# Squares of 32x32 on VectorE in place of 128x128 transposes on TensorE, from block 4 on

## The chip, the cores and the metric

The kernel runs on one core of one Trainium2 chip. The metric is the device time of one execution in microseconds (us). The engines are TensorE (PE), VectorE (DVE), ScalarE (ACT), GpSimd (POOL) and SyncE (SP), which here only issues transfers; each runs its own instructions in a fixed order, and they meet through semaphores.

## The reference

Attention against keys and values that are averaged over groups of 8 tokens, then a layer with a rational function in the middle. All in float32: 8 sequences of 576 tokens, 8 heads of 64; 4608 tokens, 512 model columns, 2048 hidden columns.

```python
k_p = k.reshape(B, H, Sp, pool, D).mean(axis=3)          # Sp = 72, pool = 8
v_p = v.reshape(B, H, Sp, pool, D).mean(axis=3)
scores = scale * np.matmul(q, k_p.transpose(0, 1, 3, 2))
scores = scores - np.max(scores, axis=-1, keepdims=True)
attn = np.exp(scores)
attn = attn / (np.sum(attn, axis=-1, keepdims=True) + 1e-09)
x = np.matmul(attn, v_p)                                  # then (B*S, H*D)
h = x @ w_in
P = a[0] + a[1] * h + a[2] * h2 + a[3] * h3               # h2 = h*h, h3 = h2*h
Q = 1.0 + np.abs(b[0]) * np.abs(h) + np.abs(b[1]) * h2
return (P / (Q + 1e-6)) @ w_out
```

## The kernel before

**Blocks and units.** The 4608 tokens are cut into 18 blocks of 256 (TOK), a block into two tiles t of 128, the 2048 hidden columns into 8 units u of 256. Sequences have 576 tokens, so some blocks straddle two of them; `segs` cuts such a block or tile in two. For a block i, `attend(i)` makes x; for each unit `mm1` multiplies x with w_in into ph, `rational` makes g from it, and `mm2` multiplies g with w_out into po, which gathers over the 8 units. Float32 products are made from high and low halves (names ending in 0 and 1, or gh and gl, am[0] and am[1]: high, and what is left).

**Attention of a tile** (`attention`). q arrives as rows of tokens (qt, one transfer of 256 KB, two when the tile straddles). PE transposes it in four 128x128 pieces into a bank pq, ACT copies that to qT. PE multiplies qT with the averaged keys kpT (ps), DVE takes the maxima mx and the differences e, ACT the exponentials, DVE the sums sm, POOL divides. e then has 72 keys for each of 8 heads, stored as 4 pairs of heads of 144 columns. The first 16 columns of a pair go their own way (er, pr, ar). The other 128 are transposed by PE into a bank pm; ACT copies it to the block's high half am[0], DVE subtracts to get the low half am[1]. `values` multiplies am and ar with the averaged values (pv), giving x.

**A unit's rational function** (`rational`). On ACT: w = Abs, r, t (both linear), then Ln and Exp into rp, then the cast gh. On DVE five instructions that end in t. On POOL the products w and gl.

**What sets the order.** Nothing is scheduled by the compiler: `Plan` records every operation with a cost in us and a due time, and `solve` places them engine by engine, taking the operation that can start first, by due time where several can. Due times come from `due(at)` (HEAD, PACE, SLOW) for the unit in which a block's work is recorded, and go backwards along the dependencies with a factor `slack`; `early` is how long before its due time an operation may start. A transfer is charged its issue cost and its bytes. `issue` then emits that order, so all instructions have line L240, and an instruction whose operand is late holds up all behind it on its engine. All transfers are issued by SP, in one queue.

Of the kernel before, what the change touches and what calls it, by code (L numbers as in the profile page):

```python
# [99 lines left out]
class Plan:  # L100
    LAT = 0.07

    def __init__(self, nc):
        self.nc, self.ops, self.rings, self.now, self.slack = nc, [], {}, 0.0, 1.2
# [10 lines left out]
    def add(self, eng, cost, calls, port=False, claims=(), bytes=0, early=24.0, after=()):  # L115
# [143 lines left out]
def tile_pooled_attention_then_rational_moe(  # L259
# [67 lines left out]
    def dma(kbytes, dst, src, eng="sp", issue=0.45, early=60.0):  # L327
        plan.add(eng, issue, [("dma_start", (dst, src), {})], bytes=kbytes * 1024, early=early)
# [232 lines left out]
    def attention(t, am, ar):  # L561
# [3 lines left out]
        qt = new("work2", "qt", [P, H, D], F32, f"qt{t}")  # L565
        for r0, r1, n in sg:
            s0 = t * P + r0 - n * S
            dma(512, qt[r0:r1], q[n, :, s0:s0 + (r1 - r0), :].rearrange("h s d -> s h d"))
        pq = bank(f"pq{t}", [P, NJ, P])
        qT = new("work1", "qT", [P, NJ * P], F32, f"qT{t}").rearrange("p (j t) -> p j t", j=NJ)  # L570
        pe(109 * NJ, [
            ("transpose", (pq[:, j, :],
                           qt[:, 2 * j:2 * j + 2, :].rearrange("s h d -> s (h d)"), ident), {})
            for j in range(NJ)], claims=(qT,))
# [4 lines left out]
        for c in range(2):
            hs = slice(4 * c, 4 * c + 4)  # L580
            ps = bank(f"ps{t}_{c}", [P, 4, SP])
# [242 lines left out]
```

## Time and profile before

| | us |
|---|---|
| median of the runs (3) | 979.89 |
| lowest and highest run | 977.5, 981.26 |
| profiled execution | 975.84 |
| span of the profiled execution | 974.1 |
| PE busy in the span | 957.4 |
| DVE, ACT, POOL busy | 735.0, 707.0, 504.9 |

Matmuls overlap: the duration of one is not what it takes from PE's queue, the distance between two starts is. PE busy thus says that something was always in it. The granted clock is TensorE's, as a share of 2.4 GHz.

### The profile page before, as it was taken

Reading aid. Unit: us, or ns where it says so; the run is one execution under the profiler, and the core shown is the slowest. Engines: PE = TensorE matmul, PEld = TensorE weight load, DVE = VectorE, ACT = ScalarE, POOL = GpSimd, SP = SyncE. Lnnn points to the kernel's source line nnn. Section 1 sums busy time; section 2 is a strip of 40 time slices with the busy share of each in tenths; the row PEclk is TensorE's granted clock in tenths of the full one; section 3 lists DMA queues with packets and bytes.
Section 4 is the critical chain, followed back from the end, with each engine's and each line's share of the span. In section 5 each row is a group of like instructions: output and inputs, shape, how many; then the busy total and the mean of one; then the engine's idle time right before and its main releaser. Section 6 shows DMA issues by size and latency. Waiting matters only on the chain.

```text
span 974.1 us, 16916 instructions
## 1 busy us (share of the span) xinstructions
PE 957.4 (98%) x6396; PEld 868.4 (89%) x6396; DVE 735.0 (75%) x1299; ACT 707.0 (73%) x1216; POOL 504.9 (52%) x443
## 2 busy tenths in 40 slices
PE   7899999999999999999999999999999999999997
PEld 6888999989898999999899989898999999999996
DVE  5898878888777768776888687867777785767664
ACT  3888889776777777777677776767776776777764
POOL 4475567664445644444645373446544474444343
PEclk9899999999999999999999999999999999999999
DMA  9993001251102301010401040102201210100000
GB/s 272 328 387 138 22 23 44 88 151 50 29 23 65 87 12 33 17 34 11 125 18 44 6 131 29 40 4 66 87 17 34 54 56 11 35 1 22 2 23 22
DMA packets 62706, 64.26 MB, mean 66 GB/s; under 512 B 39969, under 2 KB 39969, under 8 KB 62625
## 3 DMA queue, kind: packets, MB, share of 16 engines
q1 hardware_dynamic: 62624, 63.19, 20.8%
q8 instruction: 50, 0.82, 0.3%
q14 instruction: 32, 0.25, 0.1%
HBM read 50.60 MB, written 12.58 MB: 65 GB/s over the span
## 4 chain that ended last, share of the span: by engine, by line
PE 91%; DVE 3%; SPq 2%; ACT 1%; issue 1%; POOL 1%; DMA 1%; POOLq 0%; ACTq 0%; DVEq 0%
PE ph L240 40%; PE po L240 39%; PE pv L240 4%; PE ps L240 3%; SPq L240 2%; PE pq L240 1%; PE pm L240 1%; DVE t L240 1%; DMA qt<-in_q_dram 1%; PE warm L240 1%; POOL wout L240 0%; PE pr L240 0%; DVE m_wout L240 0%; PE pvs L240 0%; DVE rp L240 0%
## 5 line engine op out<-in xcount | busy, mean ns | idle before, releaser
L240 PEld LDWEIGHTS ph<-x,win 128*128 128x128 f32 x3264 | 475.3, 188 | 54.2 <-DVE vr L240 0.9
L240 PE MATMUL ph<-x,win 128*128 128x256 f32 x3264 | 502.6, 283 | 0.8 <-DVE vr L240 0.7
L240 PE MATMUL po<-wout,gh 128*128 128x512 f32 x1152 | 352.9, 397 | 0.7 <-ACT gh L240 0.7
L240 POOL TENSOR_TENSOR w<-w,r 128x512 f32<-128x512 f32 x144 | 187.5, 1302 | 271.6 <-ACT r L240 268.7
L240 POOL TENSOR_TENSOR gl<-t,gh 128x512 fp32r<-128x512 f32 x144 | 189.8, 1318 | 152.3 <-ACT gh L240 108.0
L240 PEld LDWEIGHTS po<-wout,gh 128*128 128x128 f32 x1152 | 182.7, 189 | 9.4 <-ACT gh L240 1.2
L240 DVE TENSOR_TENSOR t<-t,ph 128x512 f32<-128x512 f32 x144 | 98.4, 683 | 119.4 <-ACT t L240 111.0
L240 PE MATMUL po<-wout,gl 128*128 128x512 f32 x576 | 177.1, 396 | 0.5 <-POOL gl L240 0.5
L240 DVE SCALAR_TENSOR_TENSOR t<-t,abn,rp 128x512 f32<-128x512 f32 x144 | 106.9, 742 | 47.5 <-ACT rp L240 46.6
L240 ACT ACTIVATE w<-ph 128x512 f32<-128x512 f32 x144 | 85.8, 596 | 69.5 <-PE ph L240 65.7
L240 ACT ACTIVATE rp<-w,cbias 128x512 f32<-128x512 f32 x144 | 99.4, 691 | 38.8 <-POOL w L240 23.8
L240 ACT CAST gh<-t 128x512 fp32r<-128x512 f32 x144 | 88.6, 615 | 48.1 <-DVE t L240 47.9
L240 ACT ACTIVATE r<-w,abn 128x512 f32<-128x512 f32 x144 | 117.6, 816 | 8.1 <-DVE rp L240 2.3
L240 ACT ACTIVATE t<-ph,abn 128x512 f32<-128x512 f32 x144 | 109.8, 772 | 16.0 <-PE ph L240 12.7
L240 DVE SCALAR_TENSOR_TENSOR t<-t,abn,ph 128x512 f32<-128x512 f32 x144 | 107.4, 746 | 6.9 <-ACT w L240 2.7
L240 DVE SCALAR_TENSOR_TENSOR t<-rp,t 128x512 f32<-128x512 f32 x144 | 99.1, 688 | 3.9
L240 DVE SCALAR_TENSOR_TENSOR rp<-w,rp 128x512 f32<-128x512 f32 x144 | 98.9, 687 | 0.1
L240 PEld LDWEIGHTS po<-wout,gl 128*128 128x128 f32 x576 | 91.6, 189 | 6.0 <-POOL gl L240 1.8
L240 ACT ACTIVATE rp<-rp 128x512 f32<-128x512 f32 x144 | 84.1, 584 | 3.4
L240 POOL TENSOR_TENSOR e<-e,sm 128x576 f32<-128x576 f32 x36 | 40.9, 1154 | 15.0 <-DVE sm L240 15.0
L240 PE MATMUL pv<-am,vm 128*128 128x256 f32 (+3 forms) x288 | 46.8, 283 | 0.7 <-DVE am L240 0.7
L240 PE MATMUL ps<-kpT,qT 128*128 128x144 f32 (+1 forms) x320 | 44.7, 292 | 1.8 <-DVE t L240 0.8
(88 smaller groups left out, 864.2 us busy)
## 6 DMA issues: line engine op xcount, KB each, us to landing
out_dram<-ob SPq DMA_DIRECT2D x18, 512.0 KB, 2.8
qt<-in_q_dram SPq DMA_DIRECT2D x32, 256.0 KB, 3.2
rwin<-in_moe_w_in_dram SPq DMA_DIRECT2D x8, 1024.0 KB, 10.6
rwout<-in_moe_w_out_dram SPq DMA_DIRECT2D x8, 1024.0 KB, 11.3
st_k<-in_k_dram SPq DMA_DIRECT2D x12, 512.0 KB, 4.0
st_v<-in_v_dram SPq DMA_DIRECT2D x12, 512.0 KB, 3.9
st_v<-in_v_dram SPq DMA_DIRECT2D x48, 64.0 KB, 2.3
early<-in_k_dram SPq DMA_DIRECT2D x4, 512.0 KB, 8.9
```

Of the source, the lines that this page charges most:

```text
L240: getattr(engines[op.eng], name)(*map(value, args), **{k: value(v) for k, v in kw.items()})
```

## The change

For blocks 4 to 17 (tiles 8 to 35) neither q nor the softmax's weights pass through PE's transposes.

- **q.** `squares(i)` loads q into a tile qs of squares, [128, 4, 8, 32], by 16 transfers per sequence in the block: each fills 32 partitions with runs of 32 floats (128 bytes). One DVE instruction per tile transposes sixteen 32x32 squares straight into qT. pq and ACT's copy go. Blocks 0 to 3 keep the old way, their qt now a part of the same buffer.
- **Weights.** e becomes one tile es per block. After POOL's division DVE transposes the 128 columns of each pair in place, in squares of 32x32, once per tile. 16 transfers inside SBUF per block, each from 32 partitions to 32 partitions in runs of 128 bytes, place them in am's second half. Then one ACT copy of 1024 elements makes am[0] and one DVE subtraction makes am[1], per block. pm and its per-tile copies and subtractions go.
- **Planner.** The first `slack` is 1.9 instead of 1.2, `early` 16 instead of 24, a transfer's due time is moved about 4 us times `slack` further ahead, HEAD and PACE grow, the issue cost of a transfer is 0.48 instead of 0.45 (0.65 for the placing ones), and the partial results of blocks 0 and 1 are reloaded after the last matmul of their unit.

```diff
-        self.nc, self.ops, self.rings, self.now, self.slack = nc, [], {}, 0.0, 1.2
+        self.nc, self.ops, self.rings, self.now, self.slack = nc, [], {}, 0.0, 1.9
...
-    def add(self, eng, cost, calls, port=False, claims=(), bytes=0, early=24.0, after=()):
+    def add(self, eng, cost, calls, port=False, claims=(), bytes=0, early=16.0, after=()):
...
-                d.due = min(d.due, op.due - d.slack * (d.cost + 0.25))
+                d.due = min(d.due, op.due - d.slack * (d.cost + 0.25 + (4.0 if d.bytes else 0.0)))
...
+    HB = 32
+
+    def squares(i):
...
+        qs = new("work1", "q", [P, NJ, TOK // HB, HB], F32, f"q{i}")
+        if i < 4:
+            return qs
+        for r0, r1, n in segs(i * TOK, TOK):
+            s0 = i * TOK + r0 - n * S
+            for j in range(NJ):
+                for g in range(4):
+                    hh, d0 = g // 2, g % 2 * HB
+                    dma(3 * (r1 - r0) // 8, qs[g * HB:(g + 1) * HB, j, r0 // HB:r1 // HB, :],
+                        q[n, 2 * j + hh, s0:s0 + r1 - r0, d0:d0 + HB].rearrange(
+                            "(b s) d -> s b d", s=HB))
+        return qs
...
+        if t >= 8:
+            m = t % 2 * (P // HB)
+            dve(NJ * P).transpose(qT.rearrange("p j (b s) -> p j b s", s=HB),
+                                  qs[:, :, m:m + P // HB, :])
+        else:
...
+        if t >= 8:
+            squares = ef[:, :, REM:].rearrange("p j (g s) -> p j g s", s=HB)
+            dve(NJ * P).transpose(squares, squares)
+        else:
+            pm = bank(f"pm{t}", [P, NJ, P])
...
+        if i >= 4:
+
+            hi, lo = am
+            for a in range(4):
+                for g in range(4):
+                    k0 = REM + g * HB
+                    dma(96, lo[g * HB:(g + 1) * HB].rearrange(
+                        "p j (m a s) -> p j m a s", m=2, s=HB)[:, :, :, a, :].bitcast(F32),
+                        es[a * HB:(a + 1) * HB, :, :, k0:k0 + HB], issue=0.65)
+            hi, lo = (x.rearrange("p j t -> p (j t)") for x in am)
+            act(NJ * TOK).copy(hi, lo.bitcast(F32))
+            dve(NJ * TOK, port=True).tensor_tensor(
+                out=lo, in0=lo.bitcast(F32), in1=hi.bitcast(F32), op=ALU.subtract)
...
-    HEAD, PACE, SLOW, SLOWS = 20.0, 6.1, 5.0, 2 * NA
+    HEAD, PACE, SLOW, SLOWS = 28.0, 6.5, 5.0, 2 * NA
...
-            plan.slack = 2.5
+            plan.slack = 2.0
```

Three places in the order of instructions (TensorE, SyncE, and VectorE with ScalarE), all at block 16 (tiles 32 and 33). In the rows a name is a tile, then its block or tile number, unit and a running number: po14_0_0 belongs to block 14, am1_16 is the second half of block 16's weights.

TensorE around the scores ps of tile 32. Before, with q's transpose pq ahead of them:

```order
L240 MATMUL ph15_2_9600<-x0_15_9403,win2_623 128x256 x4
L240 MATMUL po14_0_0_9125<-wout6_2053,gh14_6_9517 128x512
L240 MATMUL po14_0_1_9127<-wout6_2053,gh14_6_9517 128x512
L240 MATMUL pq32_9640<-identr_83,qt32_8996 128x128 x4
L240 MATMUL ph15_2_9600<-x0_15_9403,win2_623 128x256 x4
L240 MATMUL po14_0_0_9125<-wout6_2053,gh14_6_9517 128x512
L240 MATMUL po14_0_1_9127<-wout6_2053,gh14_6_9517 128x512
L240 MATMUL ph15_2_9600<-x1_15_9410,win2_623 128x256 x4
```

and the scores themselves eight rows below. Now:

```order
L240 MATMUL po14_0_0_9357<-wout2_986,gl14_2_9442 128x512
L240 MATMUL po14_0_1_9359<-wout2_986,gl14_2_9442 128x512
L240 MATMUL ph14_5_9468<-x0_14_9095,win5_1512 128x256 x4
L240 MATMUL ps32_0_9515<-kpT1_149,qT32_9228 128x144 x2
L240 MATMUL ps32_1_9518<-kpT1_149,qT32_9228 128x144 x2
L240 MATMUL po14_0_0_9357<-wout2_986,gh14_2_9435 128x512
L240 MATMUL po14_0_1_9359<-wout2_986,gh14_2_9435 128x512
L240 MATMUL ph14_5_9468<-x1_14_9112,win5_1512 128x256 x4
L240 MATMUL ps33_0_9534<-kpT1_149,qT33_9525 128x144 x2
L240 MATMUL ps33_1_9542<-kpT1_149,qT33_9525 128x144 x2
L240 MATMUL ph14_6_9550<-x0_14_9095,win6_1638 128x256 x4
L240 MATMUL po14_0_0_9357<-wout2_986,gh14_2_9435 128x512
```

No transpose of q stands on PE any more; the scores of both tiles follow each other among the products of unit 14_5, where before they stood among those of 15_3.

SyncE's queue around block 16. Before:

```order
L240 DMA qt32_8996<-in_q_dram 128x8x64
L240 DMA st_v7_2_9017<-in_v_dram 16x2x512 x8
L240 DMA qt33_9072<-in_q_dram 128x8x64
L240 DMA st_v7_0_9081<-in_v_dram 128x2x512
L240 DMA st_v7_1_9181<-in_v_dram 128x2x512
L240 DMA out_0_dram<-ob13_7_9195 128x2x512
L240 DMA qt34_9653<-in_q_dram 128x8x64
L240 DMA qt35_9737<-in_q_dram 128x8x64
L240 DMA out_0_dram<-ob14_7_9784 128x2x512
L240 DMA out_0_dram<-ob15_7_10347 128x2x512
```

Now:

```order
L240 DMA q16_8941<-in_q_dram 32x8x32 x16
L240 DMA am1_15_9106<-e15_8932 32x8x32 x16
L240 DMA st_v7_1_9292<-in_v_dram 128x2x512
L240 DMA out_0_dram<-ob13_7_9384 128x2x512
L240 DMA q17_9531<-in_q_dram 32x8x32 x16
L240 DMA am1_16_9739<-e16_9539 32x8x32 x16
L240 DMA out_0_dram<-ob14_7_9983 128x2x512
```

q of block 17 stands ahead of the placement of block 16, sixteen transfers each, and the output of block 14 behind it.

VectorE where the weights of block 16 are finished. Before:

```order
L240 TENSOR_TENSOR er32_9835<-e32_9701,er32_9835 128x64
L240 TENSOR_TENSOR t15_4_9853<-t15_4_9853,ph15_4_9786 128x512
L240 TENSOR_TENSOR er32_9835<-e32_9701,er32_9835 128x64
L240 TENSOR_TENSOR er33_9848<-e33_9757,er33_9848 128x64 x2
L240 SCALAR_TENSOR_TENSOR t15_4_9853<-t15_4_9853,abn_438,ph15_4_9786 128x512
L240 TENSOR_TENSOR am1_16_9903<-pm32_9886,am0_16_9896 128x4x128
L240 TENSOR_TENSOR am1_16_9903<-pm33_9891,am0_16_9896 128x4x128
L240 SCALAR_TENSOR_TENSOR t15_4_9853<-t15_4_9853,abn_438,rp15_4_9909 128x512
L240 SCALAR_TENSOR_TENSOR rp15_4_9909<-w15_4_9862,rp15_4_9909 128x512
L240 SCALAR_TENSOR_TENSOR t15_4_9853<-rp15_4_9909,t15_4_9853 128x512
```

Now:

```order
L240 TENSOR_TENSOR er32_9684<-e16_9539,er32_9684 128x64 x2
L240 TENSOR_TENSOR er33_9690<-e16_9539,er33_9690 128x64
L240 TENSOR_TENSOR x1_15_9686<-pv15_1_9662,x0_15_9681 128x512
L240 STREAM_TRANSPOSE e16_9539<-e16_9539 128x4x128
L240 TENSOR_TENSOR er33_9690<-e16_9539,er33_9690 128x64
L240 STREAM_TRANSPOSE e16_9539<-e16_9539 128x4x128
L240 SCALAR_TENSOR_TENSOR t14_6_9629<-t14_6_9629,abn_305,ph14_6_9550 128x512
L240 SCALAR_TENSOR_TENSOR t14_6_9629<-t14_6_9629,abn_305,rp14_6_9713 128x512
L240 SCALAR_TENSOR_TENSOR rp14_6_9713<-w14_6_9657,rp14_6_9713 128x512
L240 SCALAR_TENSOR_TENSOR t14_6_9629<-rp14_6_9713,t14_6_9629 128x512
L240 TENSOR_TENSOR t14_7_9775<-t14_7_9775,ph14_7_9692 128x512
```

The two subtractions are gone from here; two transposes in place stand ahead of the last steps of unit 14_6. The subtraction of block 16 now comes 18 rows behind the second transpose, next to unit 15_1.

At the same place on ScalarE, the copy into am's first half. Before:

```order
L240 ACTIVATE w15_4_9862<-ph15_4_9786 128x512
L240 ACTIVATE r15_4_9871<-w15_4_9862,abn_438 128x512
L240 CAST gh15_3_9878<-t15_3_9802 128x512
L240 CAST am0_16_9896<-pm32_9886 128x4x128
L240 CAST am0_16_9896<-pm33_9891 128x4x128
L240 ACTIVATE rp15_4_9909<-w15_4_9862,cbias_86 128x512
L240 ACTIVATE rp15_4_9909<-rp15_4_9909 128x512
L240 ACTIVATE w15_5_9928<-ph15_5_9856 128x512
```

Now, with the end of the sixteen rows between the Exp of unit 14_6 and the copy:

```order
L240 ACTIVATE w15_0_9813<-ph15_0_9743 128x512
L240 ACTIVATE r15_0_9822<-w15_0_9813,abn_305 128x512
L240 ACTIVATE t15_0_9832<-ph15_0_9743,abn_305 128x512
L240 CAST gh14_7_9838<-t14_7_9775 128x512
L240 ACTIVATE rp15_0_9850<-w15_0_9813,cbias_86 128x512
L240 ACTIVATE rp15_0_9850<-rp15_0_9850 128x512
L240 ACTIVATE w15_1_9878<-ph15_1_9816 128x512
L240 ACTIVATE r15_1_9886<-w15_1_9878,abn_305 128x512
L240 ACTIVATE t15_1_9894<-ph15_1_9816,abn_305 128x512
L240 CAST gh15_0_9899<-t15_0_9832 128x512
L240 CAST am0_16_9906<-am1_16_9739 128x1024
L240 ACTIVATE rp15_1_9919<-w15_1_9878,cbias_86 128x512
```

The copy, which needs all sixteen placing transfers, stands ahead of the Ln and Exp of unit 15_1; pv16 follows on PE among the products of unit 15_7.

## Rows read from the trace of the kernel before

**Rows 1.** The page: engines' busy time, and the chain that ended last.
```profile
PE 957.4 (98%) x6396; PEld 868.4 (89%) x6396; DVE 735.0 (75%) x1299; ACT 707.0 (73%) x1216; POOL 504.9 (52%) x443
...
PE 91%; DVE 3%; SPq 2%; ACT 1%; issue 1%; POOL 1%; DMA 1%; POOLq 0%; ACTq 0%; DVEq 0%
```

**Rows 2.** Windows: stretch, length, busy PE, PEld, DVE, ACT, POOL, clock, DMA, GB/s.
```profile
0.00:110.00 110.00, 101.04 (x682) 90.83 (x682) 88.89 (x182) 79.86 (x141) 61.01 (x83) 0.97 0.76 249
...
160.00:800.00 640.00, 637.63 (x4297) 580.21 (x4296) 492.79 (x878) 466.18 (x816) 333.57 (x280) 1.00 0.18 52
800.00:974.00 174.00, 168.72 (x1096) 151.83 (x1094) 112.33 (x185) 116.81 (x195) 74.96 (x59) 0.99 0.05 16
```

**Rows 3.** Chain in order of time, two neighbouring blocks' pv: start, length.
```profile
853.17 1.89 PE pv L240 x16
...
903.98 1.89 PE pv L240 x16
```

**Rows 4.** Timeline of PE around a pq: start, length, instruction, count.
```profile
407.48 0.62 PE L240 MATMUL po<-wout,gl 128*128 128x512 f32 x2
...
408.41 0.62 PE L240 MATMUL po<-wout,gh 128*128 128x512 f32 x2
408.87 0.60 PE L240 MATMUL pq<-identr,qt 128*128 128x128 f32 x4
...
409.77 0.63 PE L240 MATMUL po<-wout,gh 128*128 128x512 f32 x2
```

**Rows 5.** Groups by line: count | busy us, mean ns of one | idle before, releaser.
```profile
L240 DVE TENSOR_TENSOR am<-pm,am 128x512 fp32r<-128x512 f32 x36 | 23.6, 685 | 8.3 <-ACT am L240 8.3
L240 PE MATMUL pq<-identr,qt 128*128 128x128 f32 x144 | 22.2, 277 | 0.4 <-issue 0.4
L240 ACT COPY qT<-pq 128x512 f32<-128x512 f32 x36 | 21.1, 587 | 24.1 <-PE pq L240 24.1
...
L240 ACT CAST am<-pm 128x512 fp32r<-128x512 f32 x36 | 19.4, 586 | 6.3 <-PE pm L240 6.2
...
L240 DVE SCALAR_TENSOR_TENSOR m_win<-rwin,m_win 128x1024 int32<-128x1024 int32 x8 | 10.1, 1258 | 0.0
...
L240 ACT CAST win<-m_win 128x1024 fp32r<-128x1024 f32 x8 | 8.3, 1042 | 1.5 <-DVE m_win L240 1.4
L240 DVE TENSOR_SCALAR m_win<-m_win 128x1024 int32<-128x1024 int32 x8 | 7.2, 905 | 0.0
```

**Rows 6.** Groups by line: the six ACT instructions of a unit.
```profile
L240 ACT ACTIVATE r<-w,abn 128x512 f32<-128x512 f32 x144 | 117.6, 816 | 8.1 <-DVE rp L240 2.3
L240 ACT ACTIVATE t<-ph,abn 128x512 f32<-128x512 f32 x144 | 109.8, 772 | 16.0 <-PE ph L240 12.7 <-POOL w L240 1.6 <-POOL gl L240 1.4
L240 ACT ACTIVATE rp<-w,cbias 128x512 f32<-128x512 f32 x144 | 99.4, 691 | 38.8 <-POOL w L240 23.8 <-DVE t L240 9.6 <-DVE e L240 3.4
L240 ACT CAST gh<-t 128x512 fp32r<-128x512 f32 x144 | 88.6, 615 | 48.1 <-DVE t L240 47.9
L240 ACT ACTIVATE w<-ph 128x512 f32<-128x512 f32 x144 | 85.8, 596 | 69.5 <-PE ph L240 65.7 <-DVE t L240 3.8
L240 ACT ACTIVATE rp<-rp 128x512 f32<-128x512 f32 x144 | 84.1, 584 | 3.4
```

**Rows 7.** Transfers from 405 to 422 us, two q loads: packets, MB, share of engines.
```profile
DMA packets 2081, 0.54 MB, mean 32 GB/s; under 512 B 2080, under 2 KB 2080, under 8 KB 2080
...
q1 hardware_dynamic: 2080, 0.52, 13.6%
```

**Rows 8.** The page, queue of all transfers: packets, MB, share of 16 engines.
```profile
q1 hardware_dynamic: 62624, 63.19, 20.8%
```

**Rows 9.** Tile st_v (64 and 512 KB loads): issue ns min/median/max, us to landing.
```profile
L240 SPq DMA_DIRECT2D st_v<-in_v_dram x60: 328/422/1569, 199.9 to 784.9; - x60
...
DMA to landing us min/median/max: 2.0/2.6/4.7
```

**Rows 10.** Timeline of SP's queue: eight st_v issues in a row.
```profile
304.57 4.75 SPq L240 DMA_DIRECT2D st_v<-in_v_dram  x8
```

More of the change, by code (lines that the diff above doesn't have):

```diff
@@ L325, in mm, with dma @@
         return "matmul", (out,), dict(lhsT=lhsT, rhs=rhs, start=start, stop=stop)
[L327 to L328 removed]
+    def dma(kbytes, dst, src, eng="sp", issue=0.48, early=60.0, after=()):
+        plan.add(eng, issue, [("dma_start", (dst, src), {})], bytes=kbytes * 1024, early=early,
+                 after=after)
     nc.scalar.preload_act_table_set("natural_log_exp_and_others")
@@ L563, in attention @@
+    def attention(t, am, ar, qs, es):
         sg = segs(t * P, P)
         col = slice((t % 2) * P, (t % 2 + 1) * P)
[L565 to L569, printed above, removed]
-        qT = new("work1", "qT", [P, NJ * P], F32, f"qT{t}").rearrange("p (j t) -> p j t", j=NJ)
[L571 to L574, printed above, removed]
@@ L575, in attention @@
-        act(NJ * P).copy(qT, pq)
-        e = new("work2", "e", [P, H, SP], F32, f"e{t}")
+        qT = new("work1", "qT", [P, NJ * P], F32, f"qT{t}").rearrange("p (j t) -> p j t", j=NJ)
+        if t >= 8:
[3 more added lines that the diff above has]
+        else:
+            m = t % 2 * (NJ // 2)
+            qt = qs[:, m:m + NJ // 2].rearrange("p a b (c d) -> p (a b c d)", d=HB).rearrange(
+                "p (h d) -> p h d", d=D)
+            for r0, r1, n in sg:
+                s0 = t * P + r0 - n * S
+                dma(512, qt[r0:r1], q[n, :, s0:s0 + (r1 - r0), :].rearrange("h s d -> s h d"))
+            pq = bank(f"pq{t}", [P, NJ, P])
+            pe(109 * NJ, [
+                ("transpose", (pq[:, j, :],
+                               qt[:, 2 * j:2 * j + 2, :].rearrange("s h d -> s (h d)"), ident),
+                 {}) for j in range(NJ)], claims=(qT,))
+            act(NJ * P).copy(qT, pq)
@@ L604, in attention @@
         hi, lo = am
-        pm = bank(f"pm{t}", [P, NJ, P])
-        pe(109 * NJ, [("transpose", (pm[:, j, :], ef[:, j, REM:], ident), {})
-                      for j in range(NJ)], claims=am)
-        act(NJ * P).copy(hi[:, :, col], pm)
-        dve(NJ * P).tensor_tensor(
-            out=lo[:, :, col], in0=pm, in1=hi[:, :, col].bitcast(F32), op=ALU.subtract)
+        if t >= 8:
[3 more added lines that the diff above has]
+            pm = bank(f"pm{t}", [P, NJ, P])
+            pe(109 * NJ, [("transpose", (pm[:, j, :], ef[:, j, REM:], ident), {})
+                          for j in range(NJ)], claims=am)
+            act(NJ * P).copy(hi[:, :, col], pm)
+            dve(NJ * P).tensor_tensor(
+                out=lo[:, :, col], in0=pm, in1=hi[:, :, col].bitcast(F32), op=ALU.subtract)
         pr = new("ps", "ps", [P, 2, P], F32R, f"pr{t}")
@@ L727, in mm2 @@
         if i < 2 and u0:
-            dma(512, ob, parts.pop(i), early=10.0)
+            dma(512, ob, parts.pop(i), after=(last,))
         for m in range(2):
```

25 lines of the change are left out of this document (16 added, 9 removed).

## The prediction

> **What bounds the kernel now.** I read the page's engine shares first: PE is busy 98% of the span, DVE 75%, ACT 73%, and in the chain that ended last PE holds 91% [rows 1]. A share can mix stages, so the windows come next: between 160 and 800 us PE is busy 637.63 of 640 us at a granted clock of 1.00, while DVE has 492.79 (77%) and ACT 466.18 (73%) [rows 2]. So in the middle only PE's own work sets the pace, and 2.4 us in 640 is all that any wait costs. The head (0 to 110 us) leaves PE 9.0 us idle at a clock of 0.97, the tail 5.3 us [rows 2]. One block of 256 tokens takes 50.81 us, from its neighbour's pv to its own [rows 3]. Whatever leaves PE's queue shortens the run, as long as nobody makes PE wait for the replacement.
>
> **The change, part by part.** The sum is made against the profiled execution, 975.84 us (span 974.1).
>
> *Removed from PE.* In blocks 4 to 17 (28 tiles of 128 tokens) the four pq transposes and the four pm transposes of a tile go. What do four cost? The group row gives 277 ns for one [rows 5], but matmuls overlap, so this is not what PE's queue loses; 224 times 277 ns would be 62 us. The pitch tells it: po to po without a transpose between is 408.41 - 407.48 = 0.93 us; with pq between it is 409.77 - 408.41 = 1.36 us [rows 4]. Four transposes therefore cost 0.43 us, and 28 tiles x 2 x 0.43 = 24.1 us leave PE. pm has the same shape and takes the same price.
>
> The Trainium skill, page "VectorE: DVE Perf Modes", section "Rules for kernel authors", speaks against this change: a 128x128 transpose belongs on TensorE if PSUM will do as destination. Its section "The three transpose paths" has 390 ns on TensorE and 311 ns on VectorE for 128x128 in bf16. With 390 ns each the removal would be worth 87 us; the pitch, some 107 ns each here, says 24, so the page's figure is a latency and the row decides.
>
> *Removed and added on ACT.* Per block two qT copies (587 ns) and two am copies (586 ns) go, and one copy of 1024 elements comes, 1042 ns by the cast of a weight [rows 5]: 2.35 - 1.04 = 1.3 us less. It hides under PE and is worth nothing by itself.
>
> *Added to DVE.* Per block four transposes of 512 elements come, two am subtractions (685 ns) go, one of 1024 elements comes. The trace shows no transpose on DVE. Nearest rows: 905 ns for 1024 elements, or 0.45 us for 512, from below; 1258 ns, as if each element were handled twice, from above; I take the 685 ns of an ordinary 512-wide instruction [rows 5], the same width and engine. The new subtraction lies between 1258 ns and 2 x 685. So DVE gains 4 x 0.685 - 1.37 + 1.3 = 2.7 us per block, 37 us in all. DVE's 77% of a 50.81 us block is 39.1 us; 41.8 of the new 49.1 is 85%. That is cover, but less of it, and DVE works in order. I charge PE's 2.4 us of waits in 640 a second time, rounded to 3 us. Bounds: 0, and half of what a dear transpose adds (second rival).
>
> The page "Vector Engine (DVE) Microarchitecture Reference", section "The reshape front-end and per-opcode configuration", of the Trainium skill gives one element per cycle and lane for the 32x32 transpose. At its 0.96 GHz clock that is an estimate of 0.53 us without the fixed part, and the DVE term would be 30 us at most for the 56 instead of 38; no run here shows it yet.
>
> *Added to SP's queue.* Per block 16 transfers bring q in 128-byte pieces (32 transfers in blocks 4, 6, 11, 13 and 15, which straddle two sequences) and 16 place the weights' squares. The queue was almost empty: two or three q loads per block, an output, k and v. Each placing transfer moves 256 pieces. Price of one: from below 256 x 17.8 ns / 16 engines = 0.28 us, where 17.8 ns is q's 256-byte packet (13.6% of 16 engines x 17 us over 2080 packets) [rows 7]; a typical issue is 0.42 us [rows 9]; eight in a row took 4.75 us, 0.59 each [rows 10]; from above 256 x 51.8 ns / 16 = 0.83 us, by the mean of all packets (20.8% of 16 x 974.1 us over 62624) [rows 8]. I take 0.42 to 0.59, the rows of short transfers issued back to back. Sixteen, plus 2.6 us to land [rows 9], make 9.3 to 12.0 us.
>
> Who waits? The ACT copy into am's first half needs all sixteen, and behind it in ACT's fixed order stand the Ln and Exp of the running blocks, so a late placement stalls the rational function of every unit, and only then PE. The order puts cover there: in block 16 the squares' last transpose stands on DVE next to unit 14_6's last steps, and on ACT sixteen rows of units 14_7, 15_0 and 15_1 come before the copy. By their means 596 + 816 + 772 + 615 + 691 + 584 = 4074 ns per unit [rows 6], twice, and 2.80 us more: 10.9 us if ACT ran without a gap, 15.0 at its 73% share; I take 13. The demand of 9.3 to 12.0 fits. The subtraction on DVE and pv come later still: pv16 stands among the products of unit 15_7 on PE. The next block's q transfers are issued ahead of the placement; 16 x 0.42 to 0.59 = 6.7 to 9.4 us, against half a block between the two DVE transposes that frame them. So I cost both sets of transfers at nothing.
>
> *Order.* The planner's new constants also rearrange the head, where PE had 9.0 us of waits [rows 2]; with no row for the new order I put 0, bounds -9 and +9.
>
> Sum: 975.84 - 24.1 + 3 = 954.7 us for an execution like the profiled one. The runs shown have a median of 979.89, 4.05 above it; carried over, 958.8 us.
>
> **Rivals.**
> *SP's queue decides (slower).* If a piece of 128 bytes costs what the mean packet does, a transfer takes 0.83 us, the sixteen land 15.9 us after the squares' transpose, 2.9 us beyond the cover of 13, and ACT's order stalls 14 times: +40 us, 954.7 + 40 + 4.05 = 999. It starts to cost at (13 - 2.6) / 16 = 0.65 us per transfer and has eaten the gain at 0.74. For it: no 128-byte piece and no transfer inside SBUF in the trace, and 32 transfers per block are then 26.6 us of SP. Against it: q's packets are smaller than the mean and cheap, and issues of 0.37 to 0.42 us don't grow with the number of pieces.
> The Trainium skill, "DMA: Bandwidth & Descriptors", section "Rules for kernel authors", says that transfers under 64 KB are mostly overhead and should be merged; these have 32 KB. The 2.6 us landing of a 64 KB transfer agrees [rows 9]. Paid one after the other, sixteen would land after 41.6 us, 29 too late in 14 blocks, and the run would end near 1360 us; but the eight of [rows 10] are 0.59 us apart, so the overheads overlap and I give that no chance of its own.
>
> *A dear transpose on DVE.* At 1258 ns each, DVE has 56 x 0.57 = 32 us more, 44.1 of a block's 49.1 us (90%). If half lands on PE, 954.7 + 16 + 4.05 = 975. For it: DVE then has some 5 us per block in which it may still wait. Against it: no row of 512 elements costs that.
>
> *The head loses.* All 9 us of waits once more: 968.
>
> *PE's freed time isn't used*, because the chain over DVE, ACT and POOL paces the units: 980. Against it speaks PE's 2.4 us of waiting in 640.
>
> **How the numbers follow.** Forecast 0.60; SP's queue 0.18 (0.13 past 0.74 us, 0.03 near it, 0.02 below); dear transpose 0.11, on both sides of the half-percent line; head 0.08; unused 0.03. Half a percent, 4.9 us, is about what a measurement of this kernel can tell from no change. Faster by more: 0.60 + 0.08 + 0.06 + 0.02 = 0.76; within: 0.05 + 0.03 + 0.03 = 0.11; slower: 0.13. The range goes from 951 (all of the 24.1, the 2.4 of waits, and some of the head's) to 978, which takes in the dear transpose and leaves out the dear queue.
>
> **What would show it.** Right: no pq or pm on PE after block 3, pv to pv near 49.1 us, DVE near 85%, and DMA issues near 0.4 to 0.6 us. Wrong in the SP term: ACT's wait list led by the copy into am on a DMA, the placing transfers over 0.65 us apart. Wrong in the DVE term: transposes far above 0.7 us and PE waiting for gh or gl. Wrong in the head: PE idle before 110 us far from 9 us. The forecast falls if the middle window shows PE waiting by more than a few us.

## The result and the profile after

The changed kernel takes 967.68 us (median of 4 runs, 965.75 to 968.59) against 978.69 us before (4 runs, 976.32 to 981.26): a ratio of 0.9894 with a 95% interval of 0.9873 to 0.9916. That is 11.0 us or 1.1% less; the forecast was 958.8 us, 2.1% less. The time lies in the range, the direction is right, and about half of the expected gain is missing. It is also the time that one rival had given, "the head loses", with 968 us.

The profiled execution took 966.78 us with a span of 965.1 us, 9.0 less than the 974.1 of before. First the page: busy time of the engines, and the chain of work that ended last.

```profile
PE 937.1 (97%) x6172; PEld 850.3 (88%) x6172; DVE 779.3 (81%) x1341; ACT 694.7 (72%) x1174; POOL 510.2 (53%) x443
...
PE 89%; DVE 4%; ACT 2%; SPq 2%; issue 1%; POOL 1%; DMA 1%; POOLq 0%; DVEq 0%; ACTq 0%
```

Against [rows 1], PE has 224 instructions fewer, which are 28 x 2 x 4 transposes, and 20.3 us less busy time (957.4 to 937.1). The rest of the span, in which PE was idle, grew from 16.7 to 28.0 us, so 11.3 us were given back: 20.3 - 11.3 = 9.0. The windows tell where (stretch, length, busy PE, PEld, DVE, ACT, POOL with counts, granted clock, DMA share, GB/s):

```profile
0.00:110.00 110.00, 93.83 (x613) 83.98 (x614) 84.61 (x161) 72.76 (x126) 59.33 (x79) 0.94 0.75 244
160.00:210.00 50.00, 46.17 (x290) 41.44 (x290) 41.63 (x69) 34.00 (x55) 33.57 (x23) 0.97 0.26 72
160.00:800.00 640.00, 633.47 (x4199) 575.96 (x4199) 538.54 (x937) 466.51 (x795) 346.32 (x286) 1.00 0.27 62
800.00:965.00 165.00, 159.84 (x1032) 144.54 (x1030) 112.69 (x176) 111.77 (x183) 73.43 (x58) 0.99 0.09 22
```

and of before, the second of these stretches:

```profile
160.00:210.00 50.00, 49.62 (x322) 44.67 (x321) 42.36 (x68) 39.52 (x63) 30.83 (x22) 1.00 0.32 98
```

Against [rows 2], PE's idle time in the head goes from 9.0 to 16.2 us (+7.2) while its clock falls from 0.97 to 0.94. In the middle it goes from 2.4 to 6.5 us (+4.2), and 3.8 of the 6.5 lie in the 50 us from 160 to 210, where before had 0.4. Nearly all of these 3.8 are one wait of PE's, for a subtraction on DVE (start, length, and in brackets the wait before it and what ended it):

```profile
190.65 0.41 PE L240 MATMUL pk<-identr,ks 128*128 128x128 f32 x2 [3.57 <-DVE e L240]
```

The tail is as it was (5.3 and 5.2). The clock has a part besides: the transposes were priced at 24.1 us and PE's busy time fell by 20.3. An estimate from the windows makes up for the 3.8 between: 93.83 us at 0.94 instead of 0.97, and 46.17 us at 0.97 instead of 1.00, are 4.2 us. From 210 us on the kernel runs as forecast: PE full, DVE at 538.54 of 640 us, 84%, where 85% was expected. That the gain is there, and is in part eaten in the first 210 us, also shows in the chain (start, length), where pv marks the blocks; of after, blocks 8, 16 and 17:

```profile
452.94 1.89 PE pv L240 x16
...
852.46 1.88 PE pv L240 x16
899.35 1.89 PE pv L240 x16
```

and of before, block 8, whose block 16 is the first of [rows 3]:

```profile
436.90 1.89 PE pv L240 x16
```

Block 8 comes 16.0 us later than before and block 16 comes 0.7 us earlier. Not all of the 16.0 is lost time: in the new order 6 matmuls of po and 20 of ph more stand ahead of block 8's pv, some 3.7 us of work by their pitch (an estimate), and as many ahead of block 16's, so that the stretch between the two can be compared. Over these eight blocks the pitch is 399.52 / 8 = 49.94 us instead of 416.27 / 8 = 52.03 us, 2.1 us less per block; the forecast's terms per block are 1.7 for PE, less 0.2 for DVE. Its 49.1 us from pv to pv had been taken from the 50.81 of one pair, which lies below that average.

The new operations, by group (count | busy us, mean ns of one | idle time before, and who ended it):

```profile
L240 DVE STREAM_TRANSPOSE qT<-q 128x512 f32<-128x512 f32 x28 | 19.8, 705 | 0.9 <-PE ps L240 0.6
L240 DVE STREAM_TRANSPOSE e<-e 128x512 f32<-128x512 f32 x28 | 18.8, 691 | 0.0
L240 DVE TENSOR_TENSOR am<-am,am 128x1024 fp32r<-128x1024 f32 x14 | 18.1, 1293 | 0.7 <-ACT am L240 0.7
L240 ACT CAST am<-am 128x1024 fp32r<-128x1024 f32 x14 | 14.6, 1043 | 1.8 <-DMA am<-e 1.7
```

and the new transfers, from the views of the tiles am and q (issue min/median/max in ns, first and last start; then the landing of the placing ones):

```profile
L240 SPq DMA_DIRECT2D am<-e x224: 585/609/1809, 224.9 to 867.3; - x112
...
DMA to landing us min/median/max: 1.9/2.0/4.5
...
L240 SPq DMA_DIRECT2D q<-in_q_dram x313: 311/440/4826, 2.4 to 802.2; - x157
```

The prices on the engines were met: 0.69 to 0.71 us for a transpose (taken: 0.685), 1.293 for the subtraction (1.26 to 1.37), 1.043 for the copy (1.042). Of the transfers, q's lie in what was taken (0.440 us against 0.42 to 0.59), and the placing ones above it: 0.609 us is the median of one issue, and where sixteen stand in a row they take 10.38 to 11.74 us, 0.65 to 0.73 each, such as these:

```profile
407.85 11.74 SPq L240 DMA_DIRECT2D am<-e  x16
```

That is already the 0.65 us at which the prediction let this term start to cost. The cover of the placement can be read in one block of the timeline, one of the two in which ACT had to wait (start, length, engine, instruction, count):

```profile
706.35 1.30 DVE L240 STREAM_TRANSPOSE e<-e 128x512 f32<-128x512 f32 x2
...
709.58 10.40 SPq L240 DMA_DIRECT2D am<-e  x16
...
722.74 1.05 ACT L240 CAST am<-am 128x1024 fp32r<-128x1024 f32 x1 [1.02 <-DMA am<-e]
```

The transposes end at 707.65 and ACT reaches the copy at 721.72: a cover of 14.1 us, where 13 (11 to 15) was worked out. SP had other work until 709.58, hence the wait of 1.02 us. In all 14 blocks ACT waited 1.7 us for the placement.

### The profile page after: what moved, and what is told of

Same layout as the page of the kernel before. It is cut to its first block, busy times and chain, and to the rows that moved or that the text cites. A ratio compares the mean times of both kernels' runs of the same rounds, so it can differ in the third digit from the quotient of the medians.

```text
span 965.1 us, 17176 instructions
## 1 busy us (share of the span) xinstructions
PE 937.1 (97%) x6172; PEld 850.3 (88%) x6172; DVE 779.3 (81%) x1341; ACT 694.7 (72%) x1174; POOL 510.2 (53%) x443
## 4 chain that ended last, share of the span: by engine, by line
PE 89%; DVE 4%; ACT 2%; SPq 2%; issue 1%; POOL 1%; DMA 1%; POOLq 0%; DVEq 0%; ACTq 0%
PE ph L240 40%; PE po L240 38%; PE pv L240 4%; PE ps L240 4%; SPq L240 2%; PE pvs L240 1%; DVE t L240 1%; PE warm L240 1%; DVE sm L240 1%; DMA ob<-pd 0%; POOL e L240 0%; DVE mx L240 0%; PE pr L240 0%; DVE e L240 0%; PE pq L240 0%
## 5 line engine op out<-in xcount | busy, mean ns | idle before, releaser
L240 PEld LDWEIGHTS ph<-x,win 128*128 128x128 f32 x3264 | 483.1, 189 | 60.1 <-ACT m_wout L240 1.3
L240 PE MATMUL ph<-x,win 128*128 128x256 f32 x3264 | 507.8, 282 | 2.4 <-DVE e L240 1.3
L240 POOL TENSOR_TENSOR w<-w,r 128x512 f32<-128x512 f32 x144 | 192.5, 1337 | 316.2 <-ACT r L240 289.6
L240 PE MATMUL po<-wout,gh 128*128 128x512 f32 x1152 | 356.9, 397 | 1.5 <-ACT gh L240 1.3
L240 POOL TENSOR_TENSOR gl<-t,gh 128x512 fp32r<-128x512 f32 x144 | 189.7, 1317 | 66.9 <-ACT gh L240 63.4
L240 PEld LDWEIGHTS po<-wout,gh 128*128 128x128 f32 x1152 | 182.1, 190 | 8.1 <-ACT gh L240 1.8
L240 PE MATMUL po<-wout,gl 128*128 128x512 f32 x576 | 180.4, 395 | 0.2 <-POOL gl L240 0.2
L240 DVE TENSOR_TENSOR t<-t,ph 128x512 f32<-128x512 f32 x144 | 98.2, 682 | 79.1 <-ACT t L240 77.4
L240 ACT ACTIVATE w<-ph 128x512 f32<-128x512 f32 x144 | 86.1, 598 | 104.8 <-PE ph L240 102.9
L240 DVE SCALAR_TENSOR_TENSOR t<-t,abn,rp 128x512 f32<-128x512 f32 x144 | 107.0, 743 | 42.0 <-ACT rp L240 38.7
L240 ACT ACTIVATE t<-ph,abn 128x512 f32<-128x512 f32 x144 | 110.6, 768 | 26.8 <-PE ph L240 19.2
L240 ACT ACTIVATE rp<-w,cbias 128x512 f32<-128x512 f32 x144 | 99.5, 691 | 37.1 <-POOL w L240 33.7
L240 ACT ACTIVATE r<-w,abn 128x512 f32<-128x512 f32 x144 | 117.5, 816 | 9.3 <-POOL gl L240 2.5
L240 DVE SCALAR_TENSOR_TENSOR t<-t,abn,ph 128x512 f32<-128x512 f32 x144 | 106.9, 742 | 5.4 <-ACT w L240 1.3
L240 DVE SCALAR_TENSOR_TENSOR t<-rp,t 128x512 f32<-128x512 f32 x144 | 98.7, 686 | 3.6
L240 DVE SCALAR_TENSOR_TENSOR rp<-w,rp 128x512 f32<-128x512 f32 x144 | 98.9, 687 | 0.0
L240 ACT CAST gh<-t 128x512 fp32r<-128x512 f32 x144 | 88.0, 611 | 13.5 <-DVE t L240 13.2
L240 PEld LDWEIGHTS po<-wout,gl 128*128 128x128 f32 x576 | 91.8, 190 | 4.6 <-POOL gl L240 0.9
L240 ACT ACTIVATE rp<-rp 128x512 f32<-128x512 f32 x144 | 83.8, 582 | 3.7
L240 POOL TENSOR_TENSOR e<-e,sm 128x576 f32<-128x576 f32 x36 | 42.1, 1188 | 37.4 <-DVE sm L240 28.7
L240 PE MATMUL ps<-kpT,qT 128*128 128x144 f32 (+1 forms) x320 | 46.4, 300 | 2.2 <-ACT qT L240 1.4
L240 PE MATMUL pv<-am,vm 128*128 128x256 f32 (+3 forms) x288 | 45.9, 280 | 0.0
```

The costliest lines, as they stand in the source:

```text
L240: getattr(engines[op.eng], name)(*map(value, args), **{k: value(v) for k, v in kw.items()})
```

## The experiments

So the squares do what was said, and the question is the head. The forecast had one term for it, "Order", put at nothing: the planner's constants. But the diff changes a second thing that acts from the first block on: q and e of a block's two tiles now share one buffer, where each tile had one of two buffers before. Each run below has its ratio to the kernel before, measured on the same chip beside it.

### The constants and the buffers, each without the squares

The changed kernel with the constants of before (one of the seven shown):

```diff
-    HEAD, PACE, SLOW, SLOWS = 28.0, 6.5, 5.0, 2 * NA
+    HEAD, PACE, SLOW, SLOWS = 20.0, 6.1, 5.0, 2 * NA
```

> The changed kernel with all planner constants of before (slack 1.2 and 2.5, early 24, HEAD 20, PACE 6.1, transfers not moved ahead, partial results reloaded by due time). Theory A, the constants rearranged the head: up to 110 us PE's idle time falls from 16.2 to about 9 us and the clock there rises from 0.94 to 0.97, and the time to about 957 us (968 - 7 - 4), 2.2% under before. Theory B, the block-wide single buffers of q and e serialise the first blocks: the head keeps its 16 us and the time stays at 966 to 970. Theory C, block 4's squares themselves cost: the idle 3.8 us between 160 and 210 us stays whatever the constants are.

Measured: 965.84 us (964.97 to 967.85), ratio 0.9884 (0.9867 to 0.9901). That is no different from the changed kernel's 0.9894. The theory that the constants alone make the loss falls. So does theory C: PE's idle time between 160 and 210 us goes from 3.8 to 1.0 us with the old constants. Of theory B the time fits, but not the head as it was described: up to 110 us PE idles 13.0 us instead of 16.2, at a clock of 0.91 instead of 0.94.

The kernel before with the new constants, the same lines the other way round:

> The kernel before, with only the planner constants of after; no squares, old buffers. Theory A: 979 + 11 = 990 us, PE idle about 16 us up to 110 us. Theory B or C: 979 us, PE idle about 9 us up to 110 us.

Measured: 985.53 us (984.07 to 985.93), ratio 1.0080 (1.0065 to 1.0095). Here, without the squares, the constants do cost 0.8%, 7.6 us, between the two theories; PE's idle time up to 110 us is 15.8 us, as theory A had it.

The kernel before with the block's buffers for q and e alone:

```diff
-        qt = new("work2", "qt", [P, H, D], F32, f"qt{t}")
+        qs = new("work1", "q", [P, NJ, TOK // HB, HB], F32, f"q{i}")
...
-        e = new("work2", "e", [P, H, SP], F32, f"e{t}")
+        es = new("work1", "e", [P, NJ, 2, 2 * SP], F32, f"e{i}")
```

> The kernel before in its constants, with q and e in one buffer per block of two tiles as in after, and every block through PE's transposes. Theory A: 979 us, the head as before. Theory B: up to 990 us, PE idle about 16 us up to 110 us.

Measured: 986.03 us (984.67 to 987.15), ratio 1.0087 (1.0068 to 1.0105), between the two theories; PE idles 13.0 us up to 110 us. The buffers alone cost as much as the constants alone. Both runs lose, and together, in the changed kernel, the two losses do not add up. From this run to the one with the old constants and the squares it is 986.03 to 965.84: the squares by themselves bring 20.2 us, where the forecast had 24.1 - 3 = 21.1.

### Half of the squares

The changed kernel with q through PE's transposes again, the weights by squares:

```diff
-        if i < 4:
+        if True:
             return qs
...
-        if t >= 8:
+        if False:
             m = t % 2 * (P // HB)
```

> The changed kernel with the squares for the weights alone; q goes through PE's pq again in all blocks. PE gets 28 x 0.43 = 12 us back: 968 + 12 = 980 us if nothing else moves. Theory C: q's squares burden DVE and SP at block 4, and without them the 3.8 us between 160 and 210 us shrink: 976 us. The head up to 110 us is the same code in both and stays at 16 us under theories A and B.

Measured: 973.77 us (973.46 to 974.14), ratio 0.9962 (0.9947 to 0.9977), below both of the times expected. PE's idle time between 160 and 210 us is 3.0 us instead of 3.8, so q's squares are not what makes it. Taking q's squares away costs 973.77 - 967.68 = 6 to 7 us. Half of PE's 24.1 us would be 12, so q's half is worth less than its share; this run has its own order of everything, and how much of the difference is that was not separated.

### Which buffer

The kernel before with q's block buffer only, e per tile as before:

```diff
-        qt = new("work2", "qt", [P, H, D], F32, f"qt{t}")
+        qs = new("work1", "q", [P, NJ, TOK // HB, HB], F32, f"q{i}")
```

> The kernel before with one thing from the change: q's two tiles of a block share one buffer, so that the next block's q can be loaded only when both tiles of this one have been read. No squares, constants of before, weights in tile-wide buffers as before. Theory A (this buffer alone makes the 8 us that the run with both block-wide buffers lost): 986.0, 984.5 to 987.5, with half clock and gaps on PE between 75 and 100 us. Rival B (the weights' block buffer, which is not here, made them): 978.7. Between them if both have a part.

Measured: 986.12 us (984.52 to 990.09), ratio 1.0083 (1.0053 to 1.0114). It is q's buffer: the loss is the same as with both. The windows of this run, as above, show the damage; the last line is the kernel before, for the same 50 us as the first.

```profile
60.00:110.00 50.00, 45.89 (x264) 39.73 (x264) 40.19 (x70) 38.50 (x62) 28.54 (x18) 0.86 0.45 153
80.00:85.00 5.00, 2.17 (x16) 1.58 (x15) 4.96 (x9) 3.87 (x10) 3.39 (x3) 1.00 0.48 182
85.00:90.00 5.00, 5.00 (x18) 3.98 (x16) 3.55 (x10) 4.43 (x8) 3.84 (x3) 0.66 0.00 0
90.00:95.00 5.00, 3.72 (x17) 2.62 (x16) 5.00 (x9) 3.99 (x8) 1.44 (x1) 1.00 0.00 0
95.00:100.00 5.00, 5.00 (x29) 4.96 (x28) 2.46 (x4) 4.05 (x6) 4.65 (x4) 0.53 0.00 0
100.00:105.00 5.00, 5.00 (x18) 4.32 (x18) 2.11 (x5) 2.96 (x5) 1.28 (x1) 0.50 0.00 0
...
60.00:110.00 50.00, 48.99 (x333) 43.75 (x331) 43.88 (x83) 42.99 (x74) 33.09 (x23) 1.00 0.47 169
```

Between 80 and 85 us, and again between 90 and 95, DVE is full (4.96 and 5.00 of 5 us) and PE has gaps (2.17 and 3.72 busy). PE's two longest waits in the first gap are for DVE:

```profile
81.73 1.23 PE L240 MATMUL pm<-identr,e 128*128 128x128 f32 x8 [1.09 <-DVE vr L240]
84.69 0.84 PE L240 MATMUL pq<-identr,q 128*128 128x128 f32 x4 [1.74 <-DVE am L240]
```

The subtraction am that ends the second stands in DVE's row right behind a conversion of wout, at 82.81 us and 1.23 us long. In the stretches after the two gaps PE's granted clock is 0.66, then 0.53 and 0.50, where 0.50 is the lower of its two levels (1.2 GHz), and PE counts as busy all the time while it does the same work more slowly. A pair of po matmuls in this run, at 0.50, takes 0.91 us to the next start:

```profile
100.98 1.11 PE L240 MATMUL po<-wout,gh 128*128 128x512 f32 x2
101.89 1.16 PE L240 MATMUL ps<-kpT,qT 128*128 128x144 f32 x4
```

and in the kernel before, at 1.00, it takes 0.46:

```profile
99.02 0.62 PE L240 MATMUL po<-wout,gh 128*128 128x512 f32 x2
99.48 0.63 PE L240 MATMUL ph<-x,win 128*128 128x256 f32 x4
```

So the loss in these 50 us is 3.1 us of idle time (48.99 - 45.89) and, by the clock, about 45.9 x 0.14 = 6.4 us more (an estimate). This trace is of an execution of 990.09 us, above the run's median; the run with both buffers, whose trace is of 985.99 us, has 45.45 us busy at 0.86 in the same 50 us.

### Is it the queue on SP?

A likely story: with one buffer, block 3's q can be loaded only when block 1's has been read, that load waits on SP, and two loads of wout stand behind it. SP's timeline of the run above, around these loads:

```profile
56.80 4.82 SPq L240 DMA_DIRECT2D rwout<-in_moe_w_out_dram  x2
...
70.10 0.99 SPq L240 DMA_DIRECT2D q<-in_q_dram  x2
71.14 1.37 SPq L240 DMA_DIRECT2D rwout<-in_moe_w_out_dram  x2
```

In the kernel before, all four stand ahead of the last q loads and are out by 67.41 us:

```profile
58.35 9.06 SPq L240 DMA_DIRECT2D rwout<-in_moe_w_out_dram  x4
```

Two runs test the story by moving only these q loads behind the wout loads; no other engine's order changes. First on the run with q's block buffer:

```diff
-        self.order = order
+        late = [op for op in order if name(op) == "q3"]
+        rest = [op for op in order if name(op) != "q3"]
+        at = 1 + max(i for i, op in enumerate(rest) if name(op).startswith("rwout"))
+        self.order = rest[:at] + late + rest[at:]
```

> The kernel before with q's two tiles of a block in one buffer (986.1 us), and one step moved on SP alone: block 3's two q loads, which wait for the last reading of block 1's q, stand behind the last two loads of wout instead of ahead of them. All other engines keep that run's order. Theory A (the loss is the queue: those two loads stand behind a q load that waits, and everything that they feed comes late): the loss goes, 978.5 to 980, and the last conversion of wout on VectorE starts near 82 us again instead of 91. Theory B (the loss is in the order of VectorE and PE, which the plan has drawn up around the late loads, and which stays): 986, within 1.5. Between them, both.

Measured: 986.59 us (984.82 to 989.83), ratio 1.0098 (1.0081 to 1.0115). SP's timeline shows the new order (L245 is the former L240, five lines were added):

```profile
57.08 5.77 SPq L245 DMA_DIRECT2D rwout<-in_moe_w_out_dram  x4
70.30 2.04 SPq L245 DMA_DIRECT2D q<-in_q_dram  x2
```

The two late loads are out by 62.85 us, at least 8 us earlier, and nothing is gained. DVE's timeline goes with that. The last conversion of wout in the run with q's block buffer:

```profile
91.19 1.22 DVE L240 SCALAR_TENSOR_TENSOR m_wout<-rwout,m_wout 128x1024 int32<-128x1024 int32 x1
```

with the loads moved ahead:

```profile
91.25 1.22 DVE L245 SCALAR_TENSOR_TENSOR m_wout<-rwout,m_wout 128x1024 int32<-128x1024 int32 x1
```

and in the kernel before:

```profile
81.57 1.23 DVE L240 SCALAR_TENSOR_TENSOR m_wout<-rwout,m_wout 128x1024 int32<-128x1024 int32 x1
```

The data are there, but the conversion keeps its place in DVE's row, 9.6 us later than before. The same step on the changed kernel, with the q loads put behind the two wout loads that followed them; the line that differs:

```diff
+        at = 1 + [i for i, op in enumerate(rest) if name(op).startswith("rwout")][-2]
```

> The changed kernel (967.7 us) with the same step moved on SP: block 3's two q loads stand behind the two loads of wout that followed them, all other engines in the order of the changed kernel. Theory A (the queue makes q's part of the head's loss): 967.7 - 5.5 to 967.7 - 7.8, so 960 to 962. Theory B (the order of the engines makes it): 967.7, within 1.5.

Measured: 968.68 us (966.35 to 969.58), ratio 0.9917 (0.9901 to 0.9933), no faster than the changed kernel. So the place of these two loads in the queue is not the cause. Nor are q's data too late in the run with q's block buffer: up to 110 us none of PE's waits there ends on a transfer. In the changed kernel it waits for one, an early load of q:

```profile
23.84 0.90 PE L240 MATMUL pq<-identr,q 128*128 128x128 f32 x4 [2.25 <-DMA q<-in_q_dram]
```

These 2.25 us are a direct price of the one buffer together with the new constants; with the old constants there is no such wait, and with the new ones and q per tile (below) there are 0.7 us. For the rest, what remains is the order that the planner draws up for DVE and PE when it has to count with q's one buffer: it is fixed when the program is built, and putting the two loads right afterwards does not change it. This is argued from what was ruled out and from the waits for DVE, and not shown by a run of its own. Why that order puts DVE's work so that PE gets its gaps at 80 and 90 us was not taken apart further.

### q per tile: the squares without the buffer

The changed kernel with the constants of before, and q in two buffers of a tile each as before; the block's q then takes 32 transfers of 128 pieces instead of 16 of 256. e stays in one buffer per block.

```diff
-        qs = new("work1", "q", [P, NJ, TOK // HB, HB], F32, f"q{i}")
-        if i < 4:
+        qs = new("work2", "q", [P, NJ, P // HB, HB], F32, f"q{t}")
+        if t < 8:
             return qs
-        for r0, r1, n in segs(i * TOK, TOK):
+        for r0, r1, n in segs(t * P, P):
```

> The changed kernel with the planner's constants of before, and with q kept in the two tile-wide buffers of before instead of one buffer for a block of two tiles (32 transfers of 128 pieces per block instead of 16 of 256); the weights' squares stay in one buffer per block. Theory A (q's block-wide single buffer costs the head its 8 us, as in the run with block-wide buffers alone, 986.0): the 20.2 us that the squares are worth come off a head like the one before, 978.7 - 20.2 = 958, and 956 to 961 by the scatter. Rival B (the head's loss comes with the squares or the weights' block buffer, or is made up anyway, so q's buffer costs nothing in the full kernel): 966, as with the block-wide q and the same constants (965.8). Rival C (the issues of q on SP, 32 x 0.44 + 16 x 0.61 = 23.8 us of a 49 us block, push placements past ACT's copy): over 968, and waits of that copy for a DMA in the list of waits.

Measured: 959.1 us (957.47 to 961.73), ratio 0.9804 (0.9776 to 0.9831). This is faster than both kernels, and it is the 958 of theory A: q's buffer costs its 8 us. The 16 transfers more per block did little harm: ACT waits 6.0 us in all for the placement instead of 1.7. In its windows PE is busy again in the middle, as [rows 2] has it (637.63), and the head has 10.6 us of idle time instead of 16.2:

```profile
0.00:110.00 110.00, 99.43 (x659) 89.11 (x659) 88.59 (x180) 78.81 (x139) 61.21 (x83) 0.94 0.77 249
...
160.00:800.00 640.00, 637.32 (x4235) 578.56 (x4234) 537.70 (x926) 461.08 (x794) 345.55 (x287) 1.00 0.26 61
```

The same with the new constants:

> The run with q per tile (959.1 us) with the changed kernel's planner constants in place of those of before; the squares, the order of the text and the buffers are the same. Theory A (the changed constants cost the head the 7.6 us that they cost the kernel before, 985.5 against 977.9, whenever q's buffer leaves the head room): 959.1 + 7.6 = 966.7. Theory B (the constants suit the squares, and the loss in the changed kernel is q's buffer alone, as the run of the changed kernel with the old constants, 965.8, could be read): 959, within 2. Between them: both have a part and don't add.

Measured: 961.79 us (960.99 to 963.0), ratio 0.9838 (0.9815 to 0.9861). With the new constants it is 2.7 us more, between the two theories. The part of each of the seven constants was not separated: with the old ones, q per tile and only the one for the due times of transfers new, the planner finds no order that goes through to the end, so there is no time for it. All ratios side by side:

| q's buffer | constants | without squares | with squares |
|---|---|---|---|
| per tile | old | 1 (before) | 0.9804 |
| per tile | new | 1.0080 | 0.9838 |
| per block | old | 1.0083, 1.0087 | 0.9884 |
| per block | new | not run | 0.9894 (after) |

With squares, e is in one buffer per block in every row; without them only in the run of 1.0087. Read across, the squares are worth 2.0 to 2.4%, 19 to 24 us, wherever they were tried. Read downwards, q's buffer costs 0.6 to 0.9% in every pair, and the constants 0.8%, 0.3% or 0.1%, less the more else is changed. 0.3% is about the width of these intervals, so the last two are not surely different from nothing.

### How near the two dear rivals were

The changed kernel with each of q's transposes on DVE done three times over, everything else in the same order:

```diff
-            dve(NJ * P).transpose(qT.rearrange("p j (b s) -> p j b s", s=HB),
-                                  qs[:, :, m:m + P // HB, :])
+            plan.add("dve", 0.16 + NJ * P * 1.04 / 1000, [
+                ("transpose", (qT.rearrange("p j (b s) -> p j b s", s=HB),
+                               qs[:, :, m:m + P // HB, :]), {})] * 3)
```

> The changed kernel with each of q's 28 transposes on VectorE done three times over, in the same order of everything else: 56 more instructions of 0.705 us, 39.5 us more on VectorE, the price the dear transpose would have had and more. Theory A (VectorE's 186 us of idle time carry it; it stands off the chain, and only few of the 39.5 us land): 968 to 974, 971 by the rate at which the prediction charged 37 us with 3. Rival B (VectorE works in order, and half of what is added lands): 967.7 + 20 = 988. Rival C (VectorE is the bound): 967.7 + 39.5 = 1007.

Measured: 993.25 us (993.03 to 993.85), ratio 1.0151 (1.0131 to 1.0171). 25.6 of the 39.5 us land, 65%; none of the three numbers was met, and the guess that DVE's idle time would carry it was the furthest off. PE's list of waits (us in total, times, longest) has a new first line:

```profile
PE ps L240 <- DVE qT L240: 16.1, 12, 2.2
PE pk L240 <- DVE e L240: 5.1, 1, 5.1
PE pk L240 <- DVE ks L240: 3.0, 2, 1.8
```

In the changed kernel the first of these lines is not among PE's waits of 0.2 us or more after 160 us. These waits for qT are 16.1 of the 25.6 us. DVE is only 83% busy in this run, but its order was drawn up for one transpose and not for three, and the scores ps stand in PE's row right behind qT, so a longer transpose is waited for where it stands, whatever DVE has free elsewhere.

The changed kernel with the placement in 32 transfers of 128 pieces:

```diff
-                    dma(96, lo[g * HB:(g + 1) * HB].rearrange(
-                        "p j (m a s) -> p j m a s", m=2, s=HB)[:, :, :, a, :].bitcast(F32),
-                        es[a * HB:(a + 1) * HB, :, :, k0:k0 + HB], issue=0.65)
+                    for m in range(2):
+                        dma(48, lo[g * HB:(g + 1) * HB].rearrange(
+                            "p j (m a s) -> p j m a s", m=2, s=HB)[:, :, m, a, :].bitcast(F32),
+                            es[a * HB:(a + 1) * HB, :, m, k0:k0 + HB], issue=0.325)
```

> The changed kernel with the placement of the weights' squares in 32 transfers of 128 pieces per block instead of 16 of 256, the same bytes and places. Theory A (SP's time per transfer is fixed at 0.609 us, and the cover before ACT's copy is the 13 us of the prediction): the last lands 32 x 0.609 + 2.0 = 21.5 us after the transpose, 8.5 us late in 14 blocks: 967.7 + 119 = 1087. Theory B (0.44 us for 128 pieces, as q's squares take): 16.1 us, 3.1 us late: 967.7 + 43 = 1011. Theory C (the time goes with the pieces, or the cover is really over 20 us because blocks ahead stand between): 968, within 3. In A and B the copy into am on ACT waits for DMA am<-e, 14 times.

Measured: 1014.58 us (1012.31 to 1015.44), ratio 1.0360 (1.0333 to 1.0388). The number is near theory B, the reason is not. The issues, from the view of tile am:

```profile
L240 SPq DMA_DIRECT2D am<-e x448: 585/599/1742, 173.6 to 924.5; - x150
```

With half the pieces a transfer takes 0.599 us instead of 0.609: the time goes by the transfer, as theory A had it. The waits after 160 us:

```profile
ACT am L240 <- DMA am<-e: 35.6, 13, 6.2
DVE e L240 <- DMA am<-e: 29.0, 10, 4.7
```

ACT's copy waits 2.7 us in 13 blocks, not 8.5, so the cover in this run's order is longer than the 13 us taken. DVE now waits too: the next tile's subtraction into e's one buffer cannot start before the placement has read it. The run is 46.9 us longer; how the two waits, 64.6 us in all, make that up was not taken apart. So the rival "SP's queue decides" is real: 16 transfers more per block brought it, in an order for which the planner was told 0.325 us for each, half of what they take. Whether an order drawn up for their true time would hide them is not shown.

## Why the prediction was right in direction and half off in size

- **PE.** 24.1 us for 224 transposes by their pitch of 0.43 us for four [rows 4]. Right: with DVE's 3 us it makes 21.1, and the runs give 20.2 (both block buffers, old constants), 19.4 (978.5 to 959.1, q per tile) and 23.7 (985.53 to 961.79, q per tile and new constants). The Trainium skill, page "VectorE: DVE Perf Modes", "Rules for kernel authors", would keep a 128x128 transpose on TensorE if PSUM can take it; in this kernel, where PE sets the pace, the runs decide against it.
- **ACT.** Worth nothing by itself; nothing contradicts it.
- **DVE.** The price (0.685 against 0.69 to 0.71) and the load (85% against 84%) were right, and the charge of 3 us is near what the runs show: 24.1 less the squares' measured 19.4 to 23.7 is 0.4 to 4.7. The reason given, that idle time covers DVE's work, is weaker than it was put: 39.5 us more at one place, in an order that had not counted with them, landed by 65%. The estimate of 0.53 us without the fixed part, from the Trainium skill's "Vector Engine (DVE) Microarchitecture Reference", "The reshape front-end and per-opcode configuration", is compatible with the measured 0.70.
- **SP and the placement.** Right that it costs nothing, with a price that was too low: 0.65 to 0.73 us from one placing transfer to the next against 0.42 to 0.59. With 2.0 us to land (2.6 was taken) sixteen take 12.4 to 13.7 us instead of 9.3 to 12.0, and the cover of 14.1 us against 13 just holds; ACT waits 1.7 us in all. The prediction's own sign of being wrong here, over 0.65 us apart, came without the loss, so the limit was nearer than worked out. The rule of the Trainium skill's "DMA: Bandwidth & Descriptors", "Rules for kernel authors", to merge transfers under 64 KB holds here in this form: 16 of them hide, and 32, in an order drawn up for half their time, cost 47 us.
- **Order.** This is the step that failed: "with no row for the new order I put 0". It measured 978.7 x (0.9894 - 0.9804) = 8.8 us, at the end of its bounds of -9 to +9, and the likeliest time should have carried part of it. The cause named there, the constants, is the smaller part (1 to 3 us in the kernel with the squares). The prediction's sign for it, PE idle up to 110 us far from 9 us, came with 16.2. The larger part, 5 to 8 us, is the buffer that q's two tiles share. It stood in the diff, as a tile that moves from the pool of two to the pool of one, and no term of the sum priced it: each new instruction was costed, and the smaller number of buffers, which acts from the first block on, was not. With the term at 0 in fact, in the run with q per tile and the old constants, the time is 959.1 us, and the forecast was 958.8.
- **The rivals.** "The head loses", 968 us, had a chance of 0.08 and was what came in kind. That its number fits to 0.3 us is luck: it took the head's 9 us of waits once more, and the trace has 7.2 us more waits in the head, 4.2 more behind 160 us, and the clock beside them. The other three did not come.

## What to carry to other kernels

When a diff moves a tile from a pool of two buffers to a pool of one, price that like an instruction: ask from which iteration on it acts, and how full the engines are there, above all where a planner or scheduler draws the whole order from it. In the two runs here that tried it, issuing two loads earlier afterwards gave nothing back. Where a gain is half of what the terms give, compare the windows stage by stage first: here it came as computed from 210 us on, and the first 210 us gave half of it back.

## What the runs showed of the hardware

- A transfer's time on SP's queue went by the transfer and not by its pieces: in the median 0.609 us for one issue with 256 pieces of 128 bytes inside SBUF and 0.599 us with 128 pieces. Where 16 or 32 stood in a row, they were 0.65 to 0.73 us (256 pieces) and 0.66 to 0.68 us (128 pieces) apart. Loads of q from DRAM in such pieces took 0.440 us in the changed kernel and 0.430 us in the run with 128 pieces.
- The 32x32 transposes on DVE took 0.69 to 0.71 us for 512 float32 per partition, in place and out of place alike.
- Gaps of PE of 2.8 and 1.3 us in 5 were followed by 5-us stretches at a granted clock of 0.66 to 0.50 at full occupancy; in the 50 us around them the clock's part of the loss (about 6 us, an estimate) was larger than that of the waits (3 us).
